# A gated mix of attention and a GeGLU layer: the softmax shift as a bias column, the branch turned round, and the first Q loads on another queue

## The chip, the core and the metric

The kernel runs on one core of a Trainium2 chip. The metric is the device time of one execution in microseconds, the median of three runs. A profile of one execution comes beside it, with a start and a duration for each instruction.

## What is computed

```python
x = A_x                                     # 2048 tokens x 512
# A: 32 heads of 16, one key and value head that all share
q = (x @ wq).reshape(1, 2048, 32, 16).transpose(0, 2, 1, 3)
k, v = x @ wk, x @ wv                       # 2048 x 16 each
p = softmax(einsum("bhqd,bkd->bhqk", q, k) * 16 ** -0.5)
a = einsum("bhqk,bkd->bhqd", p, v).transpose(0, 2, 1, 3).reshape(1, 2048, 512) @ wo
# B: 512 -> 1376 -> 512
b = (gelu(x @ w_gate) * (x @ w_up)) @ w_down
g = sigmoid((x * gate_w).sum(-1, keepdims=True))
out = g * a + (1 - g) * b
```

All of it is float32. `wq` and `wk` are drawn eight times larger than the other weights.

## The kernel before

Every float32 operand of the projections is split into a high and a low part of a 32-bit matmul type, and each product is made of three passes (high by high, low by high, high by low).

**Start.** For each of four groups of 512 tokens, TensorE makes the keys, values and the gate's dot product in one pass (`pk`) and the queries in four blocks of 128 rows (`pq`). `post_k` writes the keys into `kp`, `post_v` the values into `v1` and `v2`, and `post_q` writes each block of queries, high and low, to a scratch tensor `scr` in memory (L213, on SyncE's queue). VectorE keeps the largest absolute value of queries (`qmx`) and keys (`kmx`).

**Scores.** One unit `u` covers four heads over 512 tokens. `load_q` loads the unit's queries from `scr` into a tile `Q`, in two halves of partitions, 64 apart, for two heads that run side by side: 48 rows of queries (high, low, high) against 48 rows of keys (high, high, low). Behind them stand QK - KR = 3 further rows, loaded from a second scratch tensor `shs` (L285): two for a row shift in two parts, which are zero on the usual path, and a row of ones. The rows of `kp` against them are ones, ones, and a constant row. So the score matmul contracts 51 rows, and the constant row adds one number to every score. Each of the 1024 exponentials (L579) then reads a 128x1024 tile of scores in PSUM with an immediate scale and an immediate bias of 0.0.

**The shift and the branch.** `pairmax` multiplies the two maxima to a bound on the scores (`cb`), sets `flag` where the bound is over a limit, and spreads -1.01 times the bound over a row of 2048 numbers on VectorE (L318), which two transfers on ScalarE's queue (L320) put into `kp` as the constant row. The engines load `flag` (L518) and branch on it (L519). The body, for large scores, finds each row's true maximum over all scores, and puts it into `shs`; it is not entered with these inputs. A body of some 2100 TensorE instructions in the program's order, with over 1000 of VectorE and some 200 of SyncE, stands between the comparison and the code behind the join. The block of the other path holds, on TensorE and VectorE, one wait for the engine's own work, and on SyncE eight waits for all outstanding transfers, each with an addition to the semaphore, so that both paths leave the same counts.

**Attention and the GeGLU layer.** Behind the branch, an order written out by hand (`WORDS`) mixes the two. `S` and `Z` make the scores of one exponential, `V` multiplies four 128x512 tiles of exponentials by the values (L649), `F` is one step of the layer's matmuls (L358, gate and up or down projections), `H` begins a job of them and `R` ends it. Scores go through three pairs of PSUM banks: `S` uses the first two in turn, `Z` the third, which the layer's gate product `z` also uses. Exponentials are kept in twelve tiles `p`. Weights of the layer come from memory on SyncE's queue (L227), and VectorE and GpSimd split them (L127, L128). The GELU is a chain of VectorE operations (L383, L386, L387), a tanh on ScalarE (L390), and further operations on VectorE (L393 to L400). The first chunk of the layer (`g` and `u`, L343) runs ahead of the branch, beside `pairmax`.

The first two units' queries are loaded inside the start (L307), on ScalarE's queue; all later ones on SyncE's.

Of the kernel before, what the change touches and what calls it, by code (L numbers as in the profile page):

```python
# [9 lines left out]
F32 = mybir.dt.float32  # L10
F32R = mybir.dt.float32r
BF16 = mybir.dt.bfloat16
I32 = mybir.dt.int32
AF = mybir.ActivationFunctionType
ALU = mybir.AluOpType
# [4 lines left out]
P = 128  # L20
S = 2048
D = 512
H = 32
DH = 16
F = 1376
TG = 512
NTG = S // TG
# [2 lines left out]
NF = -(-F // P)  # L30
NB = 4
KR = 48
QK = 51
SCALE = DH ** -0.5
BOUND = 120.0
GC = 0.044715
# [23 lines left out]
def mix_kernel(ctx, tc, xT, wq, wkv, wo, wf, out):  # L60
    nc = tc.nc
    cp = ctx.enter_context(tc.tile_pool(name="cp", bufs=1))
    dr = ctx.enter_context(tc.tile_pool(name="dr", bufs=1, space=DRAM))
# [6 lines left out]
    def two_banks(name, i=None):  # L70
        if i is None:
            i = turn[0]
        turn.remove(i)
        turn.append(i)
        return ps_s.tile([P, 2 * TG], F32, tag=f"s{i}", name=name)

    scr = dr.tile([NTG, NB, 32, 8, TG], F32, name="scr")
    shs = dr.tile([NTG, 3, H, TG], F32, name="shs")

    kp = cp.tile([P, S], F32R, name="kp")  # L80
    v1 = cp.tile([P, NKC, 32], F32, name="v1")
# [8 lines left out]
    mm2 = cp.tile([P, 2], F32, name="mm2")  # L90
    mm1 = cp.tile([1, 2], F32, name="mm1")
    cb = cp.tile([1, 1], F32, name="cb")
    sh = cp.tile([1, 1], F32, name="sh")
    flag = cp.tile([1, 1], I32, name="flag")
    woh = cp.tile([P, NB, D], F32R, name="woh")
# [68 lines left out]
        nc.gpsimd.memset(mkb[32 * j : 32 * j + 32], 1.0)  # L164
        nc.gpsimd.memset(mkb[32 * j : 32 * j + 16], 0.0)
    make_identity(nc, ident)
    zz = woh[0:H]
    nc.gpsimd.memset(zz.bitcast(F32), 0.0)
    nc.gpsimd.memset(zz[:, 2].bitcast(F32), 1.0)
    for g in range(NTG):  # L170
        nc.gpsimd.dma_start(shs[g].rearrange("r h q -> h r q"), zz[:, 0:3].bitcast(F32))

    def passes(ps, lh, ll, rh, rl, n, first=True, last=True):
        seq = [(i, a, b) for i in range(n) for a, b in ((lh, rh), (ll, rh), (lh, rl))]
# [93 lines left out]
    Q = {}  # L268
# [6 lines left out]
            q.dma_start(t[64 * j : 64 * j + 32].bitcast(F32), scr[g, b, 0:32, hs])  # L275
            q.dma_start(t[64 * j + 32 : 64 * j + KR].bitcast(F32), scr[g, b, 0:16, hs])

    def load_q(u, shift=True, data=True, q=nc.sync):
        g, ub = divmod(u, 8)
        if data:  # L280
            Q[u] = cp.tile([P, 2, TG], F32R, tag="Q", name=f"Q{u}", bufs=2)
            load_qk(Q[u], u, q)
        if shift:
            for j in range(2):
                q.dma_start(Q[u][64 * j + KR : 64 * j + QK].bitcast(F32), shs[g, :, 4 * ub + j : 4 * ub + 4 : 2])  # L285

    fetch_w(0)
    fetch_w(1)
    for ti, tg in enumerate(order):
        xh, xl = xs[tg]  # L290
        pk = ps_a.tile([P, TG], F32, tag="pa", name=f"pk{tg}")
        passes(pk, lambda c: wkh[:, c], lambda c: wkl[:, c], lambda c: xh[:, c], lambda c: xl[:, c], NC)
        post_k(tg, pk)
        for b in range(NB):
            pq = two_banks(f"pq{tg}_{b}")[:, 0:TG]
            bs = slice(b * P, (b + 1) * P)
            passes(pq, lambda c: wqh[:, c, bs], lambda c: wql[:, c, bs], lambda c: xh[:, c], lambda c: xl[:, c], NC)
            if ti + 1 < NTG:
                split_x(order[ti + 1], b)
            post_q(tg, b, pq, ti == NTG - 1 and b == NB - 1)  # L300
            if ti == NTG - 1 and b == 0:
                for part in split_w(0):
                    part()
            if ti == NTG - 1 and b == 1:
                post_v()
            if ti == NTG - 1 and b >= 2:
                load_q(b - 2, q=nc.scalar)  # L307

    def pairmax():
        pm = two_banks("pm")[0:1, 0 : 2 * P]  # L310
        for j in range(2):
            nc.tensor.transpose(pm[:, j * P : (j + 1) * P], mm2[:, j : j + 1], ident)
        nc.vector.tensor_reduce(mm1, pm.rearrange("o (j p) -> o j p", j=2), axis=AX, op=ALU.max)
        nc.vector.tensor_mul(cb, mm1[:, 0:1], mm1[:, 1:2])
        nc.vector.tensor_scalar(flag, cb, BOUND / DH, None, op0=ALU.is_gt)
        nc.vector.tensor_scalar(sh, cb, -1.01 * DH, None, op0=ALU.mult)
        row = zz[0:1].rearrange("p a b -> p (a b)")
        nc.vector.tensor_scalar(row, row, 0.0, sh[0:1], op0=ALU.mult, op1=ALU.add)  # L318
        for r in (QK - 1, 64 + QK - 1):
            nc.scalar.dma_start(kp[r : r + 1].bitcast(F32), row.bitcast(F32))  # L320

    acc = {}
    O = {}
# [17 lines left out]
    def chain_mm(ps, terms, first=True, last=True):  # L341
        for q, (a, b) in enumerate(terms):
            nc.tensor.matmul(ps, a, b, start=(first and q == 0), stop=(last and q == len(terms) - 1),  # L343
                             skip_group_check=True)
# [29 lines left out]
    def weights_terms(n, t):  # L374
        gh, gl = W[n][:2]
        xh, xl = xs[chunks[n][0]]
        return [(w[:, t, c], x[:, c]) for c in range(NC) for w, x in ((gh, xh), (gh, xl), (gl, xh))]
# [119 lines left out]
    def run_later():  # L497
        for s in sorted(later):
            if s <= now[0]:
                for fn in later.pop(s):  # L500
                    fn()

    ps = ps_f.tile([P, TG], F32, tag="pf", name="g0")
    terms = weights_terms(0, 0)
# [1 line left out]
    pairmax()  # L506
    chain_mm(ps, terms[9:], first=False)
    up0 = ps_a.tile([P, TG], F32, tag="pa", name="u0")
    chain_mm(up0, weights_terms(0, 1))
    gelu(0, ps, lambda: up0)  # L510
    rest = split_w(1)
    for part in rest[:2]:
# [3 lines left out]
    base = now[0] + 1  # L516

    v = nc.values_load(flag[0:1, 0:1], min_val=0, max_val=1)  # L518
    with tc.If(v > 0):  # L519
        with tc.tile_pool(name="gp", bufs=1) as gp:  # L520
            zr = gp.tile([1, S], F32, name="zr")
            nc.vector.memset(zr, 0.0)
            for r in (QK - 1, 64 + QK - 1):
                nc.sync.dma_start(kp[r : r + 1].bitcast(F32), zr)
            for g in range(NTG):
                mx = gp.tile([P, 4, H, 2], F32, tag="mx", name=f"mx{g}")
                for ub in range(8):
                    t = gp.tile([P, 2, TG], F32R, tag="gq", name=f"gq{g}_{ub}", bufs=2)
                    load_qk(t, 8 * g + ub, nc.sync)
                    for i in range(4):  # L530
                        for h in range(4):
                            rs = slice(64 * (h % 2), 64 * (h % 2) + KR)
                            for e in range(2):
                                ps = two_banks("gs")
                                for j in range(2):
                                    k0 = e * 1024 + j * 512
                                    nc.tensor.matmul(ps[:, j * 512 : (j + 1) * 512],
                                                     t[rs, h // 2, i * P : (i + 1) * P],
                                                     kp[rs, k0 : k0 + 512], start=True, stop=True)
                                nc.vector.tensor_reduce(mx[:, i, 4 * ub + h, e : e + 1], ps, axis=AX, op=ALU.max)  # L540
                m1 = gp.tile([P, 4, H], F32, tag="m1", name=f"m1{g}")
                nc.vector.tensor_reduce(m1, mx, axis=AX, op=ALU.max)
                pt = ps_f.tile([P, TG], F32, tag="pf", name=f"pt{g}")
                for i in range(4):
                    nc.tensor.transpose(pt[0:H, i * P : (i + 1) * P], m1[:, i], ident)
                nm = gp.tile([H, TG], F32, tag="nm", name=f"nm{g}")
                nb = gp.tile([H, 3, TG], F32R, tag="nb", name=f"nb{g}")
                nc.vector.tensor_scalar(nm, pt[0:H], -1.0, None, op0=ALU.mult)
                nc.vector.memset(nb[:, 2].bitcast(F32), 1.0)
                nc.vector.tensor_copy(nb[:, 0], nm)  # L550
                nc.vector.tensor_sub(nb[:, 1], nm, nb[:, 0])
                nc.sync.dma_start(shs[g].rearrange("r h q -> h r q"), nb.bitcast(F32))
            load_q(0, data=False)
            load_q(1, data=False)


# [5 lines left out]
    def scores(n, third):  # L562
        s, pr = divmod(n, 2)
        if s >= nsteps:
            now[0] += 1
            run_later()
            return
        u, kc = divmod(s, NKC)
        now[0] = base + n
        if pr == 0 and kc == 2 and u >= 1 and u + 1 < 8 * NTG:  # L570
            load_q(u + 1)
        run_later()
        ps = two_banks("s", 2 if third else next(i for i in turn if i < 2))
        for j in range(2):
            rs = slice(64 * j, 64 * j + QK)
            nc.tensor.matmul(ps[:, j * TG : (j + 1) * TG], kp[rs, kc * P : (kc + 1) * P],  # L576
                             Q[u][rs, pr], start=True, stop=True)
        p = m2.tile([P, 2 * TG], F32, tag="p", name="p", bufs=PB)
        nc.scalar.activation(p, ps, AF.Exp, bias=0.0, scale=SCALE)  # L579
        pb[s, pr] = p  # L580

    def norm(u):
# [136 lines left out]
    g = NTG - 1  # L719
# [50 lines left out]
```

## Time and profile before

| | |
|---|---|
| median of 3 runs | 1263.01 us (1261.27 to 1263.29) |
| the profiled execution: its span, the only time that its page gives | 1262.1 us |
| TensorE busy | 1248.1 us, 99% of the span, 9884 matmuls |
| ScalarE busy | 1031.1 us, 82% |
| VectorE busy | 572.8 us, 45% |
| GpSimd busy | 221.7 us, 18% |
| the 1024 exponentials (L579) | 979.8 us busy, 1025 ns each |
| mean granted TensorE clock | 0.996 |

In the lines of the profile, PE is TensorE's matmuls, PEld its weight loads, DVE VectorE, ACT ScalarE, POOL GpSimd, SP SyncE; a `q` behind the name is the engine's sequencer or its DMA queue. Groups of instructions have their line, engine, operation, tiles and shapes and count, then busy time in us and the mean of one in ns, then the idle time of the engine ahead of them and what ended it. Rows of the timeline have start and duration in us, and in brackets the idle time before. Matmuls are pipelined and their ends modelled, so a busy TensorE is not TensorE at its peak.

### The profile page before, as it was taken

How to read it: one execution, taken by the hardware profiler on the slowest of the kernel's cores; microseconds unless marked ns; L12 is line 12 of the kernel's file. 1: busy time of each engine (PE TensorE's matmuls, PEld its weight loads, DVE VectorE, ACT ScalarE, POOL GpSimd, SP SyncE). 2: the span in 40 equal slices, each digit the busy share in tenths (PEclk: the TensorE clock that was granted, in tenths of full speed). 3: DMA queues.
4: the chain of work that ended last, by engine and by line, in shares of the span. 5: the costliest groups of instructions: out<-in, count | busy, mean ns of one | idle time of the engine just before them, and what ended most of it. 6: DMA issues, size and time to landing. Idle time of an engine off the chain costs nothing.

```text
span 1262.1 us, 23901 instructions
## 1 busy us (share of the span) xinstructions
PE 1248.1 (99%) x9884; PEld 669.8 (53%) x9884; DVE 572.8 (45%) x860; ACT 1031.1 (82%) x1118; POOL 221.7 (18%) x261
## 2 busy tenths in 40 slices
PE   9989999999999999999999999999999999999998
PEld 6855555555455555545555555554544555455454
DVE  6762352635453163453546146362546324445334
ACT  5358888888898888888888888888887888888893
POOL 3132211201320020211131012120232002112100
PEclk9989999999999999999999999999999999999999
DMA  8441111111210111211030021011111013011000
GB/s 316 163 159 56 40 42 49 39 39 56 81 39 14 63 61 39 64 39 56 23 97 2 31 81 64 16 63 39 47 53 63 15 31 106 22 43 39 15 1 34
DMA packets 26371, 72.67 MB, mean 58 GB/s; under 512 B 4016, under 2 KB 4048, under 8 KB 26256
## 3 DMA queue, kind: packets, MB, share of 16 engines
q1 hardware_dynamic: 25244, 69.17, 16.5%
q8 instruction: 80, 1.31, 0.4%
q10 hardware_dynamic: 756, 1.11, 0.3%
q0 software_dynamic: 256, 0.79, 0.2%
q14 instruction: 35, 0.29, 0.1%
HBM read 57.67 MB, written 13.37 MB: 56 GB/s over the span
## 4 chain that ended last, share of the span: by engine, by line
PE 92%; ACT 1%; DVE 1%; issue 0%; POOL 0%; ACTq 0%
PE acc L649 37%; PE s L576 23%; PE z L358 18%; PE y L358 13%; ACT p L579 1%; PE wos L343 1%; DVE acc L466 0%; PE wof L343 0%; DVE sq L386 0%; POOL mark L366 0%; DVE sq L387 0%; DVE gs L394 0%; DVE n L600 0%; DVE gs L383 0%; ACT sq L390 0%
## 5 line engine op out<-in xcount | busy, mean ns | idle before, releaser
L579 ACT ACTIVATE p<-s 128x1024 f32<-128x1024 f32 x1024 | 979.8, 1025 | 176.2 <-PE s L576 169.0
L649 PE MATMUL acc<-p,v 128*32 128x512 f32 x4096 | 490.8, 598 | 0.0
L576 PE MATMUL s<-Q,kp 51*128 51x512 f32 x2048 | 392.2, 420 | 5.9 <-SPq L519 3.2
L576 PEld LDWEIGHTS s<-Q,kp 51*128 51x128 f32 x2048 | 188.1, 185 | 247.9 <-ACT p L579 167.5
L649 PEld LDWEIGHTS acc<-p,v 128*32 128x32 f32 x4096 | 107.7, 109 | 246.7 <-issue 241.1
L128 POOL TENSOR_TENSOR gl<-st,gh 128x512 fp32r<-128x512 f32 x88 | 123.9, 1429 | 400.1 <-PE s L576 177.4
L383 DVE COPY gs<-z 128x512 f32<-128x512 f32 x43 | 29.8, 692 | 247.6 <-PE z L358 124.6
L358 PE MATMUL y<-xh,gh 64*128 64x512 f32 x344 | 138.9, 404 | 1.5 <-DVE gs L394 1.5
L358 PE MATMUL z<-xh,gh 64*128 64x512 f32 x344 | 139.0, 404 | 0.7 <-POOL mark L366 0.7
L358 PE MATMUL z<-xl,gh 64*128 64x512 f32 x344 | 135.7, 394 | 0.0
L358 PE MATMUL y<-xl,gh 64*128 64x512 f32 x344 | 135.5, 394 | 0.0
L358 PE MATMUL y<-xh,gl 64*128 64x512 f32 x344 | 135.2, 393 | 0.0
L358 PE MATMUL z<-xh,gl 64*128 64x512 f32 x344 | 135.1, 393 | 0.0
L366 POOL MEMSET mark<- 1x1 f32 x81 | 8.5, 104 | 585.6 <-PE y L358 583.6
L456 DVE SCALAR_TENSOR_TENSOR acc<-z,gc,acc 128x512 f32<-128x512 f32 x24 | 18.0, 751 | 146.5 <-PE z L358 106.0
L358 PEld LDWEIGHTS z<-xh,gh 64*128 64x128 f32 x344 | 64.6, 188 | 16.0 <-POOL mark L366 8.8
L358 PEld LDWEIGHTS z<-xh,gl 64*128 64x128 f32 x344 | 64.3, 187 | 8.9
L358 PE MATMUL z<-dh,hh 64*128 64x512 f32 x176 | 69.0, 392 | 0.0
L358 PE MATMUL z<-dh,hl 64*128 64x512 f32 x176 | 68.9, 392 | 0.0
L358 PE MATMUL y<-dh,hh 64*128 64x512 f32 x176 | 68.9, 391 | 0.0
L358 PE MATMUL y<-dh,hl 64*128 64x512 f32 x176 | 68.8, 391 | 0.0
L358 PEld LDWEIGHTS z<-xl,gh 64*128 64x128 f32 x344 | 64.8, 188 | 7.6
(147 smaller groups left out, 1583.4 us busy)
## 6 DMA issues: line engine op xcount, KB each, us to landing
st<-wf SPq DMA_DIRECT2D x44, 768.0 KB
scr<-q SPq DMA_DIRECT2D x16, 512.0 KB
Q<-scr SPq DMA_DIRECT2D x60, 128.0 KB
out<-acc SPq DMA_DIRECT2D x16, 256.0 KB
Q<-scr SPq DMA_DIRECT2D x60, 64.0 KB
xr<-xT SPq DMA_DIRECT2D x6, 512.0 KB
xst<-xT SPq DMA_DIRECT2D x12, 256.0 KB
xr<-xT SPq DMA_DIRECT2D x4, 256.0 KB
```

What stands on the lines that cost most here:

```text
L128: eng_l.tensor_sub(lo, src, hi)
L343: nc.tensor.matmul(ps, a, b, start=(first and q == 0), stop=(last and q == len(terms) - 1), skip_group_check=True)
L358: mm = nc.tensor.matmul(ps, a[rs], b[rs], start=(half == 0 and q == 0), stop=(half == 1 and q == len(X) - 1), skip_group_check=True)
L366: relay = nc.gpsimd.memset(mark, 0.0).ins
L383: nc.vector.tensor_copy(gs, g)
L456: nc.vector.scalar_tensor_tensor(o, ps, w, o, op0=ALU.mult, op1=ALU.add)
L576: nc.tensor.matmul(ps[:, j * TG : (j + 1) * TG], kp[rs, kc * P : (kc + 1) * P], Q[u][rs, pr], start=True, stop=True)
L579: nc.scalar.activation(p, ps, AF.Exp, bias=0.0, scale=SCALE)
L649: nc.tensor.matmul(accp[u][32 * j : 32 * j + 32], vt[:, kc], pb[s, j // 2][:, (j % 2) * TG : (j % 2 + 1) * TG], start=(kc == 0), stop=(kc ...
```

## The change

It has three parts.

1. The shift leaves the keys. QK goes from 51 to 50, `shs` and the loads from it have two rows instead of three, and the row operation L318 and the two transfers L320 are gone. `pairmax` computes one number `sh`, already scaled; a new function `spread` multiplies a row of 128 ones by it on TensorE, which puts it on all partitions of a PSUM tile, and VectorE copies it to a 128x1 tile `bias`. `spread` stands behind nine of the twelve matmuls of `u0`. The exponentials read `bias` instead of the immediate 0.0. In the body the rows of zeros are replaced by clearing `bias`.
2. The branch is asked to fall through to the block of the false case. In the program's order this block now stands directly behind the comparison, and the body behind it.
3. The first two units' Q loads are issued on SyncE's queue, as the later ones are.

```diff
-QK = 51
+QK = 50
...
-    shs = dr.tile([NTG, 3, H, TG], F32, name="shs")
+    shs = dr.tile([NTG, 2, H, TG], F32, name="shs")
...
+    ones = cp.tile([1, P], F32, name="ones")
+    bias = cp.tile([P, 1], F32, name="bias")
...
-    zz = woh[0:H]
+    nc.gpsimd.memset(ones, 1.0)
+    zz = woh[0:H, 0:2]
     nc.gpsimd.memset(zz.bitcast(F32), 0.0)
-    nc.gpsimd.memset(zz[:, 2].bitcast(F32), 1.0)
     for g in range(NTG):
-        nc.gpsimd.dma_start(shs[g].rearrange("r h q -> h r q"), zz[:, 0:3].bitcast(F32))
+        nc.gpsimd.dma_start(shs[g].rearrange("r h q -> h r q"), zz.bitcast(F32))
...
             if ti == NTG - 1 and b >= 2:
-                load_q(b - 2, q=nc.scalar)
+                load_q(b - 2)
...
-        nc.vector.tensor_scalar(sh, cb, -1.01 * DH, None, op0=ALU.mult)
-        row = zz[0:1].rearrange("p a b -> p (a b)")
-        nc.vector.tensor_scalar(row, row, 0.0, sh[0:1], op0=ALU.mult, op1=ALU.add)
-        for r in (QK - 1, 64 + QK - 1):
-            nc.scalar.dma_start(kp[r : r + 1].bitcast(F32), row.bitcast(F32))
+        nc.vector.tensor_scalar(sh, cb, -1.01 * DH * SCALE, None, op0=ALU.mult)
+
+    def spread():
+        pm = two_banks("ps")[:, 0:1]
+        nc.tensor.matmul(pm, ones, sh, start=True, stop=True)
+        nc.vector.tensor_copy(bias, pm)
...
-    chain_mm(up0, weights_terms(0, 1))
+    terms = weights_terms(0, 1)
+    chain_mm(up0, terms[:9], last=False)
+    spread()
+    chain_mm(up0, terms[9:], first=False)
     gelu(0, ps, lambda: up0)
...
-    with tc.If(v > 0):
+    with tc.If(v > 0, preferred_fallthrough_block=False):
         with tc.tile_pool(name="gp", bufs=1) as gp:
-            zr = gp.tile([1, S], F32, name="zr")
-            nc.vector.memset(zr, 0.0)
-            for r in (QK - 1, 64 + QK - 1):
-                nc.sync.dma_start(kp[r : r + 1].bitcast(F32), zr)
+            nc.vector.memset(bias, 0.0)
...
-        nc.scalar.activation(p, ps, AF.Exp, bias=0.0, scale=SCALE)
+        nc.scalar.activation(p, ps, AF.Exp, bias=bias, scale=SCALE)
```

The lines left out make the tiles of the body two rows instead of three, and drop two arguments of `load_q` that are no longer used.

More of the change, by code (lines that the diff above doesn't have):

```diff
@@ L276, in load_qk, with load_q @@
             q.dma_start(t[64 * j + 32 : 64 * j + KR].bitcast(F32), scr[g, b, 0:16, hs])
-    def load_q(u, shift=True, data=True, q=nc.sync):
+    def load_q(u, data=True):
         g, ub = divmod(u, 8)
+        q = nc.sync
         if data:
@@ L282, in load_q @@
             load_qk(Q[u], u, q)
-        if shift:
-            for j in range(2):
-                q.dma_start(Q[u][64 * j + KR : 64 * j + QK].bitcast(F32), shs[g, :, 4 * ub + j : 4 * ub + 4 : 2])
+        for j in range(2):
+            q.dma_start(Q[u][64 * j + KR : 64 * j + QK].bitcast(F32), shs[g, :, 4 * ub + j : 4 * ub + 4 : 2])
     fetch_w(0)
```

3 lines of the change are left out of this document (1 added, 2 removed).

## The prediction

> **What bounds the kernel now.** I read the page first, then the list of waits, then busy time by stage, then the timeline.
>
> ```profile
> PE 1248.1 (99%) x9884; PEld 669.8 (53%) x9884; DVE 572.8 (45%) x860; ACT 1031.1 (82%) x1118; POOL 221.7 (18%) x261
> PE 92%; ACT 1%; DVE 1%; issue 0%; POOL 0%; ACTq 0%
> L579 ACT ACTIVATE p<-s 128x1024 f32<-128x1024 f32 x1024 | 979.8, 1025 | 176.2 <-PE s L576 169.0
> L576 PEld LDWEIGHTS s<-Q,kp 51*128 51x128 f32 x2048 | 188.1, 185 | 247.9 <-ACT p L579 167.5
> ```
>
> TensorE is busy nearly all the time and carries 92% of the chain that ended last (second line), with ScalarE at 1%. That looks like a kernel in which ScalarE, at 82%, has room. The list of waits says how thin the room is:
>
> ```profile
> ACT p L579 <- PE s L576: 169.0, 240, 8.2
> PEld s L576 <- ACT p L579: 167.5, 215, 1.2
> ```
>
> ScalarE waits for scores 240 times in 1024 exponentials, and the weight loads of the scores wait for an exponential 215 times, since a score bank is free again only once its exponential has read it. So the lead passes back and forth: 1024 / 240 = 4.27 exponentials make one streak without a wait for scores, and 215 waits against 240 streaks is about one wait of TensorE in each. By stage (us, then busy time of PE, PEld, DVE, ACT, POOL with counts, granted clock, DMA):
>
> ```profile
> 69.50:82.00 12.50, 7.96 (x42) 7.00 (x44) 6.26 (x12) 5.54 (x7) 4.19 (x4) 0.73 0.45 137
> 82.00:1262.00 1180.00, 1172.56 (x9562) 611.10 (x9558) 517.13 (x767) 996.80 (x1063) 201.54 (x222) 1.00 0.14 46
> ```
>
> The first row is the stage around the branch, the second the attention. The change touches the first by its branch, and the second by one operand of each exponential. What a streak looks like:
>
> ```profile
> 88.05 5.58 ACT L579 ACTIVATE p<-s 128x1024 f32<-128x1024 f32 x6
> 93.82 2.90 ACT L579 ACTIVATE p<-s 128x1024 f32<-128x1024 f32 x3 [0.19 <-PE s L576]
> 97.30 2.96 ACT L579 ACTIVATE p<-s 128x1024 f32<-128x1024 f32 x3 [0.59 <-PE s L576]
> ...
> 90.02 0.30 PEld L576 LDWEIGHTS s<-Q,kp 51*128 51x128 f32 x4 [1.18 <-ACT p L579]
> 93.22 0.19 PEld L576 LDWEIGHTS s<-Q,kp 51*128 51x128 f32 x2 [0.84 <-ACT p L579]
> ```
>
> In the streak of six TensorE waits for ScalarE, the last time at 93.22, behind the fifth exponential; in the two streaks of three it does not. Longer exponentials would there pass on the addition of 5 in 12.
>
> **Part 1: the bias becomes an operand in memory.** In the program of before, each exponential carries its bias as an immediate 0.0; in the changed one it reads `bias`, a 128x1 tile in SBUF. The removed key row saves nothing: a score matmul streams the same 512 columns with 50 rows as with 51. No activation of before reads such an operand, so its price is bounded by neighbours:
>
> ```profile
> L383 DVE COPY gs<-z 128x512 f32<-128x512 f32 x43 | 29.8, 692 | 247.6 <-PE z L358 124.6 <-PE y L358 123.0
> L454 DVE TENSOR_SCALAR acc<-z,gc 128x512 f32<-128x512 f32 x8 | 6.0, 751 | 51.8 <-PE z L358 51.8
> L394 DVE SCALAR_TENSOR_TENSOR gs<-y,sq 128x512 f32<-128x512 f32 x43 | 29.8, 692 | 4.0
> L456 DVE SCALAR_TENSOR_TENSOR acc<-y,gc,acc 128x512 f32<-128x512 f32 x24 | 17.8, 743 | 0.0
> L194 DVE COPY v<-pv 128x256 f32<-128x256 f32 x1 | 0.4, 408 | 0.0
> L702 DVE TENSOR_SCALAR gt<-gt 128x16 f32<-128x16 f32 x1 | 0.2, 176 | 0.0
> L700 ACT ACTIVATE gt<-zt 128x16 f32<-128x16 f32 x1 | 0.2, 207 | 0.0
> L390 ACT ACTIVATE sq<-sq 128x512 f32<-128x512 f32 x44 | 27.7, 629 | 1.2 <-DVE sq L387 1.1
> ```
>
> On VectorE the same size costs 692 ns with immediates (L383, L394) and 751 or 743 ns where a column of scalars is read (L454, L456): 55 ns more. To carry that over I scale by the fixed cost of an instruction. By the 16-element rows that is 207 ns on ScalarE against 176: 55 x 207 / 176 = 65 ns. By the slope between two sizes it is 629 - 512 x (1025 - 629) / 512 = 233 ns on ScalarE against 408 - 256 x (692 - 408) / 256 = 124 on VectorE: 55 x 233 / 124 = 103 ns. I take the middle, 84 ns. The outer ends are 0 (fetched under the instruction before) and 207 ns (a whole fixed cost again); a gain is excluded, since an operand is added. *The Trainium skill, page "ScalarE: Activation LUTs", section "What ACT_TABLE_LOAD costs", prices an ACTIVATE with immediates at 186 ns + 0.833 ns an element and adds about 93 ns for each [128,1] pointer operand. For 1024 elements the first figure gives 1039 ns, the trace has 1025; no run here shows the second. By 93 ns the sum below would be 1307.0.*
>
> All of it does not reach the end. 1024 x 0.084 = 86 us is less than the 1180.00 - 996.80 = 183 us in which ScalarE is idle in the attention stage, so ScalarE does not become the bound everywhere. An addition passes on only as far as the last place in a streak at which TensorE waits; behind it ScalarE's own wait absorbs it. The 215 waits say one such place in each streak but not where; I take the middle: 215 x 4.27 / 2 = 459 exponentials, 45% (the window above has 42%). **459 x 0.084 = 38.6 us.** A place a third into the streak gives 306 exponentials, two thirds gives 612. An addition of 4.27 x 0.084 = 0.36 us for each streak against a mean idle of 169.0 / 240 = 0.70 us joins some streaks, which speaks for the upper half.
>
> **Part 2: the branch.** The rows of the branch's line, engine by engine (count, ns, start):
>
> ```profile
> L519 DVEq COMPARE_BRANCH  x1: 72/72/72, 68.1 to 68.1; - x1
> L519 PEldq COMPARE_BRANCH  x1: 3892/3892/3892, 68.1 to 68.1; - x1
> L519 SPq COMPARE_BRANCH  x1: 45/45/45, 68.4 to 68.4; - x1
> ...
> L519 SPq EVENT_SEMAPHORE  x8: 17/17/17, 71.7 to 72.5; - x8
> L519 DVEq EVENT_SEMAPHORE  x1: 21/21/21, 71.3 to 71.3; - x1
> L519 PEldq EVENT_SEMAPHORE  x1: 51/51/51, 72.1 to 72.1; - x1
> ```
>
> On engines with a long body the jump takes 3.9 us (TensorE), 71.3 - 68.1 = 3.2 us (VectorE) and 71.7 - 68.4 = 3.3 us (SyncE). In the program's order the jump over the body stays: before, the comparison jumps to the other block, which stands behind the body; after, it falls into that block, but the block ends in an unconditional branch, and the body still lies between it and the code that follows. What moves is the wait. That block holds, on TensorE and VectorE, a wait for the engine's own work: now done after the jump, then ahead of it.
>
> ```profile
> L312 PE MATMUL pm<-ident,mm 128*1 128x128 f32 x2 | 0.4, 272 | 0.0
> ...
> 69.11 0.39 PE L343 MATMUL u<-xh,gl 128*128 128x512 f32 x1
> 72.65 0.70 PE L576 MATMUL s<-Q,kp 51*128 51x512 f32 x2 [3.15 <-SPq L519]
> ...
> 73.67 0.43 PE L358 MATMUL y<-xh,gl 64*128 64x512 f32 x1
> 75.49 0.80 PE L576 MATMUL s<-Q,kp 51*128 51x512 f32 x2 [1.39 <-issue]
> ```
>
> Before, TensorE's jump began at 68.1, under queued matmuls that ran to 69.50. After, it begins at 69.50 plus some 0.2 for the new matmul of `spread` (an estimate from the two small ones on L312, 0.4 us together) and ends at 69.7 + 3.9 = 73.6; with 0.4 us of waits behind it, taken from 72.1 to the matmul at 72.65 without the wait for SyncE, the first scores come at 74.0: **+1.3 us**. Ends: 0 (if part of the 3.9 us was itself a wait for the queue to drain) and 1.7. The stall of 1.39 us at 75.49 and the half clock after it move along at no change.
>
> ```profile
> L318 DVE TENSOR_SCALAR woh<-woh,sh 1x2048 fp32r<-1x2048 f32 x1 | 1.3, 1274 | 0.1
> ...
> 68.85 0.74 DVE L127 CAST gh<-st 128x512 fp32r<-128x512 f32 x2
> 71.45 0.76 DVE L127 CAST dh<-st 128x512 fp32r<-128x512 f32 x1 [1.87 <-DVEq L519]
> 72.85 1.67 DVE L387 SCALAR_TENSOR_TENSOR sq<-sq,gs 128x512 f32<-128x512 f32 x1
> ...
> 76.32 1.03 ACT L579 ACTIVATE p<-s 128x1024 f32<-128x1024 f32 x1 [1.15 <-PE s L576]
> 81.62 0.76 DVE L127 CAST gh<-st 128x512 fp32r<-128x512 f32 x2
> ```
>
> VectorE loses the 1.27 us row operation (L318), but its copy to `bias` waits for `spread`, which stands behind nine of the twelve u matmuls; queued behind it are the copy of g, the splits of `gh` on which GpSimd waits, and the jump. With `spread` three matmuls of 0.23 us ahead of the end of u, so near 68.8, the copy of `bias` at about 69.1, then 0.69 and 0.74 us, they end near 70.5 instead of 68.85 + 0.74 = 69.59, and VectorE resumes at 70.5 + 3.2 = 73.7 instead of 71.45.
>
> `sq` then ends at 74.52 + 2.3 = 76.8 and the tanh at 77.4; the second exponential waits for its scores until 76.3 + 1.3 = 77.6 anyway. Without that cover of 0.2 us the rest would be added. The Q loads, twelve transfers, leave ScalarE's queue, where nothing computes then, and stand on SyncE's behind and ahead of the last `scr` write; SyncE takes them, then the flag, then waits until all have landed, before 73.6 by the old chain, which ended before 72.65 with two key-row transfers more. SyncE then jumps, so the next weight loads start some 3 us later than before; they are first read at 81.62, eight microseconds behind the join: nothing.
>
> **Sum.** The profiled span is 1262.1, the median 1263.01 of runs from 1261.27 to 1263.29; 0.9 lies around the span, and I add to the median: 1263.0 + 38.6 + 1.3 = **1302.9**.
>
> **Rivals.** *The idle absorbs it*: the operand is fetched under the instruction before, or the 86 us fit into ScalarE's 183 us. For: the chain's 1%. Against: the 215 waits of TensorE on ScalarE. Then 1263.0 + 1.3 = 1264.3.
>
> *ScalarE paces everything*: all streaks join and every exponential counts: 1263.0 + 86 + 1.3 = 1350. For it the idle would have to lie where no lead can be kept; against it stand the streaks of three above, with idle time between them.
>
> ```profile
> 75.50:78.00 2.50, 2.50 (x12) 2.50 (x13) 2.21 (x4) 1.03 (x1) 0.00 (x0) 0.50 0.92 263
> 78.00:80.50 2.50, 2.50 (x14) 2.50 (x13) 0.00 (x0) 1.36 (x2) 0.00 (x0) 0.50 0.39 159
> ```
>
> *Faster, the jump goes*: if the fall-through spares the long jump, TensorE waits only for the Q loads: until about 71.5, an estimate from SyncE's first semaphore of the join at 71.7, 1.15 us sooner; the 1.39 us stall goes, and the half clock, 5.0 us of work at a granted clock of 0.50, gives back 2.5 us. That is 1263.0 - 5.0 = 1258, and it decides only if the operand costs under 5.0 / 459 = 11 ns. Against it: the body still has to be jumped. *The Trainium skill, page "Runtime: NRT & Kernel Launch", section "Instruction fetch mechanics", says that a taken branch out of the two pages held forces a fetch by DMA before execution goes on; the 3.9 us above agree, and by that rule an unconditional jump over the same body pays again.*
>
> **Chances.** Forecast 0.84, absorbed 0.08, all on ScalarE 0.06, faster 0.02. The forecast's range: 65 ns on 306 exponentials, 19.9 us, gives 1283; 103 ns on 612, 63.0, with 1.7 at the branch gives 1328. I leave out the rivals and a little of the forecast, about 0.2. A measurement of this kernel tells 0.2%, 2.5 us, from no change. Faster 0.02; same 0.07, the absorbed case nearly whole; slower 0.91.
>
> **What would show it.** Right: L579's mean at about 1109 ns instead of 1025, ScalarE's busy time up by some 86 us, its idle before L579 well under 176.2, more waits of the score loads for ScalarE, and the first scores near 74.0. Wrong: a mean still at 1025 (part 1 falls); a mean up but the span not (the absorption is complete); or no compare-and-jump gap near 70 to 73 us (part 2 falls).

## The result, and the profile after

The changed kernel takes 1284.42 us, median of 5 runs (1283.90 to 1286.47), against 1263.01 for the kernel before (5 runs, 1260.49 to 1263.29): 21.4 us slower. The ratio, taken over all runs, is 1.018 (95% interval 1.0167 to 1.0192); that of the two medians is 1.017. The forecast was 1302.9 us, in a range from 1283 to 1328. The direction and the two places were as forecast; the larger term came out at a little over half its size.

The page of the changed kernel: busy time and share of the engines, the chain that ended last, and the exponential's group with the idle time of ScalarE ahead of it; below them, from the list of waits, the two waits between TensorE and ScalarE (us, times, longest).

```profile
PE 1268.3 (99%) x9886; PEld 660.6 (52%) x9886; DVE 571.0 (45%) x860; ACT 1110.9 (87%) x1118; POOL 221.0 (17%) x261
PE 91%; ACT 1%; DVE 1%; issue 0%; POOL 0%; DMA 0%; ACTq 0%; POOLq 0%
L581 ACT ACTIVATE p<-s,bias 128x1024 f32<-128x1024 f32 x1024 | 1063.3, 1118 | 117.5 <-PE s L578 114.5
```

```profile
PEld s L578 <- ACT p L581: 233.4, 457, 1.4
ACT p L581 <- PE s L578: 114.5, 194, 9.6
```

Each exponential takes 1118 ns instead of 1025. ScalarE's busy time rose by 1110.9 - 1031.1 = 79.8 us, its idle time before the exponential fell from 176.2 to 117.5 us, and by the list of waits the weight loads of the scores wait for it 457 times, where it had 215. The chain still gives ScalarE 1%, though ScalarE's instruction is what grew. By stage (length, then busy time of PE, PEld, DVE, ACT and POOL with counts, granted clock, DMA share, GB/s):

```profile
69.50:82.00 12.50, 8.63 (x42) 6.35 (x44) 5.68 (x10) 5.76 (x7) 4.05 (x4) 0.59 0.37 134
82.00:1282.70 1200.70, 1192.08 (x9562) 602.29 (x9558) 517.23 (x767) 1076.48 (x1063) 202.19 (x222) 1.00 0.13 45
```

The attention stage grew from 1180.00 to 1200.70 us with the same 1063 instructions on ScalarE: nearly all of the loss. ScalarE's idle time in it was 1180.00 - 996.80 = 183.2 us and is now 1200.70 - 1076.48 = 124.2 us. So of 79.7 us of added work 59 went into idle time, and 20.7 came out as time. The traced execution of the kernel before has a stretch at half clock in this stage (the row below, with a granted clock of 0.50) that the changed kernel's and most others here don't have:

```profile
957.95:961.36 3.41, 3.41 (x20) 2.66 (x18) 3.41 (x4) 1.77 (x3) 3.03 (x2) 0.50 0.00 0
```

The exponentials of the traces without it gain about 1.55 us on those of before at that place, so that the stage of before is longer by this much than theirs would be, and the growth without it is 22.3 us. What the prediction showed as three streaks reads now:

```profile
88.19 9.18 ACT L581 ACTIVATE p<-s,bias 128x1024 f32<-128x1024 f32 x9
97.74 3.13 ACT L581 ACTIVATE p<-s,bias 128x1024 f32<-128x1024 f32 x3 [0.37 <-PE s L578]
101.30 2.12 ACT L581 ACTIVATE p<-s,bias 128x1024 f32<-128x1024 f32 x2 [0.44 <-PE s L578]
```

The streak of six and the next one of three have joined to nine. From its start to that of the streak behind it are 9.55 us, where it was 97.30 - 88.05 = 9.25: nine exponentials with 0.093 us each more, 0.84 us, moved the next streak by 0.30. The idle of 0.19 us between the two streaks is gone, and 0.22 of the 0.59 us before the third. Where the time stands on TensorE, by the score matmuls' group (busy, mean | idle), before and after:

```profile
L576 PE MATMUL s<-Q,kp 51*128 51x512 f32 x2048 | 392.2, 420 | 5.9 <-SPq L519 3.2 <-issue 1.4 <-ACT p L579 1.3
```

```profile
L578 PE MATMUL s<-Q,kp 50*128 50x512 f32 x2048 | 410.3, 437 | 7.0 <-SPq L525 3.8 <-ACT p L581 2.5 <-issue 0.6
```

18.1 us more busy and 1.1 us more idle, together 19.2. So the loss stands in hardly any idle column, and the page shows TensorE at 99% in both kernels. Score matmuls come in two lengths: nearly all those of over 0.45 us (0.49 us on average) start together with a weight load of the scores, which had not been done ahead, and the others take 0.39 us. Counted in the traces from 82 us on, 512 of some 2036 are long in the kernel before, 926 in the changed one. They run in pairs, so that 207 more pairs at 0.1 us each are about 20.7 us (an estimate, since the ends of matmuls are modelled).

Around the branch: the rows of its line by engine (count, shortest, median and longest ns, first and last start), then TensorE's, VectorE's and ScalarE's timeline (start, duration, in brackets the idle time before).

```profile
L525 SPq EVENT_SEMAPHORE  x8: 17/17/17, 71.6 to 72.1; - x8
L525 PEldq COMPARE_BRANCH  x2: 95/1730/3364, 66.5 to 69.1; - x2
L525 DVEq COMPARE_BRANCH  x2: 51/53/55, 68.7 to 69.6; - x2
L525 PEldq EVENT_SEMAPHORE  x1: 51/51/51, 68.9 to 68.9; - x1
```

```profile
68.51 0.40 PE L346 MATMUL u<-xh,gl 128*128 128x512 f32 x1
72.73 0.89 PE L578 MATMUL s<-Q,kp 50*128 50x512 f32 x2 [3.83 <-SPq L525]
73.42 0.62 PE L361 MATMUL y<-xh,gh 64*128 64x512 f32 x1
75.54 0.80 PE L578 MATMUL s<-Q,kp 50*128 50x512 f32 x2 [0.64 <-issue]
```

```profile
68.04 0.16 DVE L323 COPY bias<-ps 128x1 f32<-128x1 f32 x1 [2.21 <-PE ps L322]
72.44 0.43 DVE L129 CAST dh<-st 128x512 fp32r<-128x512 f32 x1 [2.98 <-issue]
```

```profile
75.19 0.63 ACT L393 ACTIVATE sq<-sq 128x512 f32<-128x512 f32 x1 [0.36 <-DVE sq L390]
76.38 1.11 ACT L581 ACTIVATE p<-s,bias 128x1024 f32<-128x1024 f32 x1 [0.56 <-PE s L578]
```

On TensorE the comparison now takes 95 ns, the wait for its own work ends at 68.9, at the end of u, and only then an unconditional branch (the longer of the two COMPARE_BRANCH rows) begins at 69.1 and takes 3364 ns. VectorE, too, compares and jumps. TensorE's gap is 3.83 us instead of 3.15. The clock: 0.59 over these 12.5 us is 2 x 0.41 x 12.5 = 10.3 us at half, where before 0.73 was 6.8 us.

### The profile page after: what moved, and what is told of

It reads as the page before. It is cut to its first block, busy times and chain, and to the rows that moved or that the text cites. A ratio compares the mean times of both kernels' runs of the same rounds, so it can differ in the third digit from the quotient of the medians.

```text
span 1282.7 us, 23905 instructions
## 1 busy us (share of the span) xinstructions
PE 1268.3 (99%) x9886; PEld 660.6 (52%) x9886; DVE 571.0 (45%) x860; ACT 1110.9 (87%) x1118; POOL 221.0 (17%) x261
## 4 chain that ended last, share of the span: by engine, by line
PE 91%; ACT 1%; DVE 1%; issue 0%; POOL 0%; DMA 0%; ACTq 0%; POOLq 0%
PE acc L651 36%; PE s L578 24%; PE z L361 17%; PE y L361 13%; ACT p L581 1%; PE wos L346 1%; DMA xst<-xT 0%; DVE acc L469 0%; POOL gl L130 0%; PE wof L346 0%; DVE ol L627 0%; DVE xh L129 0%; POOL xl L130 0%; DVE sq L389 0%; DVE sq L390 0%
## 5 line engine op out<-in xcount | busy, mean ns | idle before, releaser
L581 ACT ACTIVATE p<-s,bias 128x1024 f32<-128x1024 f32 x1024 | 1063.3, 1118 | 117.5 <-PE s L578 114.5
L578 PE MATMUL s<-Q,kp 50*128 50x512 f32 x2048 | 410.3, 437 | 7.0 <-SPq L525 3.8
L578 PEld LDWEIGHTS s<-Q,kp 50*128 50x128 f32 x2048 | 186.0, 184 | 300.6 <-ACT p L581 233.4
L361 PE MATMUL z<-dh,hl 64*128 64x512 f32 x176 | 68.9, 392 | 0.0
L361 PE MATMUL y<-dh,hl 64*128 64x512 f32 x176 | 68.9, 392 | 0.0
L361 PE MATMUL z<-dh,hh 64*128 64x512 f32 x176 | 68.8, 391 | 0.0
```

Source lines behind the costliest of these rows:

```text
L361: mm = nc.tensor.matmul(ps, a[rs], b[rs], start=(half == 0 and q == 0), stop=(half == 1 and q == len(X) - 1), skip_group_check=True)
L581: nc.scalar.activation(p, ps, AF.Exp, bias=bias, scale=SCALE)
```

## The experiments

All times are medians; each set shares its runs of the kernel before. "Ratio" is against that kernel over all runs, so that it can differ a little from that of the two medians.

| kernel | what it is | us | before | ratio, 95% interval |
|---|---|---|---|---|
| ptr_only | before, a zero tile as bias | 1283.31 | 1261.88 | 1.0167, 1.0153 to 1.0181 |
| after_imm | after, immediate 0.0 as bias | 1265.19 | 1261.88 | 1.0023, 1.0013 to 1.0033 |
| ptr_half | zero tile in every second exponential | 1266.14 | 1261.88 | 1.0035, 1.0023 to 1.0048 |
| ptr_double | tiles for bias and scale | 1332.61 | 1261.88 | 1.0558, 1.0544 to 1.0572 |
| ptr_ffn | zero tile where the layer's work follows | 1270.33 | 1261.43 | 1.0074, 1.0060 to 1.0088 |
| ptr_attn | zero tile in the others | 1269.55 | 1261.43 | 1.0066, 1.0052 to 1.0080 |
| branch_only | before, fall-through turned round | 1263.30 | 1261.43 | 1.0015, 1.0006 to 1.0024 |
| q_only | before, first Q loads on SyncE | 1265.93 | 1261.43 | 1.0038, 1.0024 to 1.0051 |
| no_shift | before without any shift | 1264.36 | 1261.66 | 1.0018, 1.0009 to 1.0027 |
| no_shift_q | no_shift, first Q loads on SyncE | 1263.35 | 1261.66 | 1.0007, 0.9998 to 1.0016 |
| fill_only | before, 12 matmuls ahead of the jump | 1263.03 | 1261.66 | 1.0013, 1.0004 to 1.0022 |
| no_shift_fill | no_shift with the 12 matmuls | 1265.16 | 1261.66 | 1.0031, 1.0021 to 1.0042 |

**The operand alone, and all but the operand.**

```diff
# ptr_only, against before
+    zb = cp.tile([P, 1], F32, name="zb")
+    nc.gpsimd.memset(zb, 0.0)
-        nc.scalar.activation(p, ps, AF.Exp, bias=0.0, scale=SCALE)
+        nc.scalar.activation(p, ps, AF.Exp, bias=zb, scale=SCALE)
# after_imm, against after
-        nc.scalar.activation(p, ps, AF.Exp, bias=bias, scale=SCALE)
+        nc.scalar.activation(p, ps, AF.Exp, bias=0.0, scale=SCALE)
```

> The kernel before, with one edit: the exponentials read a 128x1 tile of zeros as bias instead of the immediate 0.0; the key row, the branch and the Q loads stay as before. Theory A, the operand carries the whole change: L579-type exponentials at 1118 ns as in the changed kernel, time 1263 + 20 to 22 us. Rival B, branch and Q loads carry a part: under 1263 + 17 us.

> The changed kernel with the immediate 0.0 back as bias of the exponentials; bias is still computed and not read, so no shift is applied on the usual path (exp of unshifted scores). Theory A: exponentials at 1025 ns and a time within 1.5 us of 1263, since the branch, by the two traces, moves nothing by 82 us. Rival B: 1266 or more, the part that branch and Q loads cost. Prediction's part 2 by itself: 1264.3.

The exponential's group in ptr_only, then in after_imm, and after_imm's TensorE around the branch:

```profile
L581 ACT ACTIVATE p<-s,zb 128x1024 f32<-128x1024 f32 x1024 | 1063.3, 1119 | 117.1 <-PE s L578 113.6 <-ACT p L581 0.5 <-PE y L360 0.5
```

```profile
L581 ACT ACTIVATE p<-s 128x1024 f32<-128x1024 f32 x1024 | 980.6, 1025 | 176.3 <-PE s L578 159.7 <-DVE sq L389 9.6 <-ACT p L581 0.8
```

```profile
69.35 0.40 PE L346 MATMUL u<-xh,gl 128*128 128x512 f32 x1
73.53 0.89 PE L578 MATMUL s<-Q,kp 50*128 50x512 f32 x2 [3.79 <-issue]
```

The operand alone makes 1.67 of the 1.8%, with the group's mean within one nanosecond of the changed kernel's; whose tile it is doesn't matter. Theory A holds there. Without the operand the rest of the change costs 0.23%, 2.9 us, which is between what the two theories had (up to 1264.5, from 1266), and TensorE's gap of 3.79 us at the branch is there as in the changed kernel. (0.0167 and 0.0023 add up to 0.019; the changed kernel has 0.018, within the intervals.)

**The dose.** ptr_half gives the tile to every second exponential; ptr_double gives a second tile, for the scale, to all.

```diff
# ptr_half
+        nc.scalar.activation(p, ps, AF.Exp, bias=zb if n % 2 else 0.0, scale=SCALE)
# ptr_double
+    nc.gpsimd.memset(sc, SCALE)
+        nc.scalar.activation(p, ps, AF.Exp, bias=zb, scale=sc)
```

> The kernel before; every second exponential reads the tile of zeros as bias, the others the immediate. Theory linear (a fixed share of 22% of each addition passes on): + 10 us. Theory convex (the idle behind each streak takes a small addition first): + 4 to 7 us. The prediction's share of 45% would give + 21 us.

> The kernel before; all exponentials read both the bias (zeros) and the scale from 128x1 tiles. If a second operand costs as much as the first, 1211 ns each. Theory linear: + 41 us. Theory convex: the first 93 ns ate 59 us of ScalarE's 183 us of idle, the second finds less to eat, + 55 to 75 us. If the second operand is read beside the first at no cost, 1118 ns and + 21 us.

Groups by form, the attention stage and the weight loads' wait of ptr_half; the exponential's and the score matmuls' group and the stage of ptr_double:

```profile
L581 ACT ACTIVATE p<-s,zb 128x1024 f32<-128x1024 f32 x512 | 572.6, 1118 | 48.9 <-PE s L578 45.8 <-ACT p L581 0.4
L581 ACT ACTIVATE p<-s 128x1024 f32<-128x1024 f32 x512 | 525.7, 1027 | 93.0 <-PE s L578 91.6 <-PE y L360 0.6 <-ACT p L581 0.2
```

```profile
82.00:1264.30 1182.30, 1173.81 (x9548) 606.34 (x9544) 515.98 (x765) 1032.37 (x1062) 201.23 (x222) 1.00 0.14 46
```

```profile
PEld s L578 <- ACT p L581: 160.3, 279, 1.6
```

```profile
L583 ACT ACTIVATE p<-s,zb,sc 128x1024 f32<-128x1024 f32 x1024 | 1147.7, 1209 | 80.9 <-PE s L580 75.3 <-PE y L362 0.5 <-ACT p L583 0.2
L580 PE MATMUL s<-Q,kp 51*128 51x512 f32 x2048 | 430.4, 449 | 21.0 <-ACT p L583 8.4 <-SPq L523 3.1 <-issue 0.4
```

```profile
82.00:1330.80 1248.80, 1225.90 (x9550) 595.89 (x9547) 516.02 (x765) 1160.23 (x1062) 200.22 (x222) 1.00 0.14 43
```

The price is a property of the single instruction: 1118 and 1027 ns side by side, and the second tile adds another 1209 - 1119 = 90 ns. The time isn't proportional to it. ScalarE's added work in the stage is 35.6, 79.7 and 163.4 us (half, changed kernel, double), and ScalarE's idle time falls from 183.2 to 149.9, 124.2 and 88.6. The time of the stage rises by 2.3, 20.7 and 68.8; with the 1.55 us at half clock that only the trace of before has, by some 3.9, 22.3 and 70.4. The share that comes out as time is then 11% of the first 36 us, 42% of the next 44 and 57% of the next 84.

**Where an exponential stands.** ptr_ffn gives the tile to the 543 exponentials behind which a layer's step (`F`, `H` or `R`) comes, ptr_attn to the other 481.

```diff
# ptr_ffn (ptr_attn: not in)
+            ctx[0] = (toks[at + 1 : at + 2] or ["V"])[0][0]
+        nc.scalar.activation(p, ps, AF.Exp, bias=zb if ctx[0] in "FHR" else 0.0, scale=SCALE)
```

> The kernel before; the tile of zeros is read as bias by the 543 exponentials whose word is followed by a step of the layer's matmuls (F, H or R), the other 481 keep the immediate. Theory V (ScalarE paces where values and scores stand close together): + 0 to 4 us, less than half of the 21.4. Rival F (S F3 costs TensorE 0.99 us per exponential against 0.92 on ScalarE, so there the room is smallest): + 10 us or more.

> The counterpart: the 481 exponentials followed by V, S or Z read the tile of zeros, the 543 others the immediate. Theory V: + 8 to 16 us, most of the 21.4. Rival F: + 0 to 4 us. If neither place matters and only the load does (theory convex alone): both about + 4 to 5 us, as for every second exponential.

The stage and the weight loads' wait in ptr_ffn, then in ptr_attn:

```profile
82.00:1267.30 1185.30, 1177.28 (x9540) 602.99 (x9536) 515.29 (x764) 1034.86 (x1061) 200.39 (x221) 1.00 0.14 45
```

```profile
PEld s L579 <- ACT p L582: 208.0, 382, 1.4
```

```profile
82.00:1267.80 1185.80, 1177.33 (x9540) 606.32 (x9537) 515.32 (x764) 1030.56 (x1060) 200.30 (x221) 1.00 0.14 45
```

```profile
PEld s L579 <- ACT p L582: 186.2, 290, 1.7
```

Both theories fall: the two sets cost the same, 0.74% and 0.66%. But each costs about twice what ptr_half does (0.35%, intervals apart), with about as many slow exponentials, so that the third guess, that only their number counts, falls too. What differs is that here the slow ones are neighbours: in ptr_half each stands alone, in ptr_ffn all but 7 and in ptr_attn all but 64 have a slow one beside them. That additions pass on where they pile up within a few exponentials, because the three pairs of score banks give a lead of two or three, fits this and the convex dose; it is argued from these times, and no run varied the number of banks.

**The branch, and the queue.**

```diff
# branch_only, against before
-    with tc.If(v > 0):
+    with tc.If(v > 0, preferred_fallthrough_block=False):
# q_only, against before
-                load_q(b - 2, q=nc.scalar)
+                load_q(b - 2)
```

> The kernel before with the fall-through of the branch alone turned. Prediction's part 2: the wait for the engine's own work stands ahead of the jump, first scores 1 to 1.4 us after TensorE's gap would have ended, time + 1 to 3 us. Rival, the jump goes: - 3 to - 5 us and no gap of 3 us.

> The kernel before with the first two units' Q loads on SyncE's queue alone; branch, key row and immediate as before. Theory: 0 within 1 us, since the transfers land before the jump is over either way; ScalarE's two key-row transfers then start right behind pairmax instead of behind the Q loads. Rival: the loads land later and the first scores with them, + 1 to 2 us.

branch_only: TensorE's branch rows and its timeline. q_only: SyncE's queue (the transfers' issues), what its wait ended on, and TensorE's first scores.

```profile
L519 PEldq COMPARE_BRANCH  x2: 95/1780/3464, 67.4 to 68.9; - x2
```

```profile
68.35 0.39 PE L343 MATMUL u<-xh,gl 128*128 128x512 f32 x1
72.77 0.74 PE L576 MATMUL s<-Q,kp 51*128 51x512 f32 x2 [4.03 <-DVE dh L127]
```

```profile
67.25 0.77 SPq L276 DMA_DIRECT2D Q<-scr  x1
71.91 0.30 SPq L275 DMA_DIRECT2D Q<-scr  x1
```

```profile
SPq L275 <- DMA kp<-woh: 3.9, 1, 3.9
```

```profile
77.58 1.06 PE L576 MATMUL s<-Q,kp 51*128 51x512 f32 x2 [8.78 <-SPq L519]
```

Turned round alone, the branch costs 0.15%, 1.9 us, and TensorE's gap is 4.03 us instead of 3.15. In the two traced executions, which have the same stretches at half clock up to there, the last exponentials start only 0.3 us apart, so the traces show less of a loss than the medians do. The Q loads alone cost 0.38%, 4.8 us, which none of the theories had: SyncE issues nothing from 68.0 to 71.9, while its load waits 3.9 us for a key-row transfer of ScalarE's queue (`kp<-woh`), and the first scores come at 77.58.

**Without the shift.** no_shift removes the row, its transfers and its VectorE operations and adds nothing: 50 rows, immediate 0.0. It leaves out the common shift, which cancels in the softmax. no_shift_q moves the Q loads in it.

```diff
# no_shift, against before (no_shift_q: also load_q(b - 2))
-QK = 51
+QK = 50
-        nc.vector.tensor_scalar(row, row, 0.0, sh[0:1], op0=ALU.mult, op1=ALU.add)
-        for r in (QK - 1, 64 + QK - 1):
-            nc.scalar.dma_start(kp[r : r + 1].bitcast(F32), row.bitcast(F32))
```

> The kernel before without any shift: the immediate 0.0 as bias, no constant row in keys and queries (50 rows instead of 51), no transfer of the key rows from ScalarE's queue and no matrix product that spreads the shift; the branch and ScalarE's queue for the first Q loads are as before. It leaves out the common shift (which cancels in the softmax).
> Theory P (the operand alone costs the 21 us; what the row of the keys did before was worth little): 1262 (1259.5 to 1263.5), no more than the few tenths that the two key-row transfers and their three small VectorE operations take before the first scores, and the exponential stays at 1025 ns.
> Theory K (the key row itself costs time, by its 51st row in 900 score matmuls or by its transfers ahead of the first scores, so that moving the shift brings something that the operand's price hides): under 1259, with a score matmul mean well under 420 ns or first scores over 1 us earlier than 72.65.

> no_shift with the first Q loads on SyncE's queue, as in the changed kernel. With the key-row transfers still there, the same move alone took +4.5 us: SyncE's queue stood from 68.0 to 71.9 ahead of the third load of Q1, and the first scores came at 77.6.
> Theory L (that load waits for the semaphore that the first key-row transfer from ScalarE, issued at 67.65, is counted on; without the transfers there is nothing to wait for): within 1 us of no_shift; SyncE's Q loads are issued without a gap over 1 us until about 68.7, and the first scores come within 1 us of those of no_shift.
> Theory W (SyncE's queue itself is late: the stores of q and the Q loads on one queue): +3.5 to +5 us against no_shift, the gap before the third load is there again, first scores near 77.

no_shift's score matmuls; then SyncE's queue in no_shift_q and its and TensorE's branch rows:

```profile
L563 PE MATMUL s<-Q,kp 50*128 50x512 f32 x2048 | 392.1, 420 | 6.1 <-SPq L511 3.4 <-issue 1.6 <-ACT p L566 1.1
```

```profile
67.59 0.82 SPq L274 DMA_DIRECT2D Q<-scr  x1
68.45 0.45 SPq L273 DMA_DIRECT2D Q<-scr  x1
```

```profile
L511 PEldq COMPARE_BRANCH  x1: 4692/4692/4692, 67.7 to 67.7; - x1
L511 SPq COMPARE_BRANCH  x1: 45/45/45, 71.0 to 71.0; - x1
```

```profile
74.48 0.94 PE L563 MATMUL s<-Q,kp 50*128 50x512 f32 x2 [4.84 <-SPq L511]
```

The row brings nothing when it goes: a score matmul has 420 ns with 50 rows as with 51. Theory K falls. Theory P is right on the exponential, but no_shift is 0.18% slower than before, 0.9 us above the forecast range. Set side by side, in two traces that both have the half-clock stretch near 958 us, the exponentials of no_shift start level with those of before until the 88th (0.05 us apart) and fall behind by 1.6 us over the rest: 0.3 us at the 500th, 0.8 at the 700th. With that stretch allowed for, the other kernels with 50 rows and the immediate drift by 1.1 to 1.5 us from the 88th to the last, and those with 51 (branch_only, q_only, fill_only) by 0.4 to 0.5, so that part of the drift belongs to this execution of before. The rest is open.

In no_shift_q SyncE's loads are issued without the gap, so theory L is right on its cause: the load waited for the key-row transfer, as q_only's list of waits says too. The first scores still come at 74.48, 1.8 us behind no_shift's 72.67, because SyncE reaches its own jump only at 71.0, after the loads and the flag; the median is 1.0 us below no_shift's.

**The clock behind the jump.**

```diff
# fill_only, against before; no_shift_fill has the same
+    fill = two_banks("wz", 2)[:, 0:TG]
+    for _ in range(12):
+        nc.tensor.matmul(fill, warm[:, 0:P], warm, start=True, stop=True)
```

> The kernel before with 12 more 128x512 bf16 matmuls on a warm-up tile into a bank that is free, between the last projection matmul and the jump: TensorE's clock record has no gap of over 3 us before the first scores. It adds work whose result is not read.
> Theory H (the 6.8 us at half clock after the jump come from the 3.15 us in which TensorE has no matmul, and cost about 2.5 us net of the matmuls put in): 1260.5 (1259 to 1262), with the half clock after the jump gone or one window of 3.4 us shorter.
> Theory J (the gap is the instruction fetch of the jump itself, and comes after the fill as it came before): 1263 to 1266, the same gap of 3 us and the same half clock, shifted by the fill's length of up to 3 us.

> no_shift and fill together. Theory H with P: 1259.5 (1258 to 1262), the first scores at about the time of no_shift, and no or less half clock after them. Theory J: no_shift's time plus 0 to 3 us, half clock as before.

fill_only: TensorE's jump and the wait behind it, its timeline and the stage around the branch.

```profile
L522 PEldq COMPARE_BRANCH  x1: 3812/3812/3812, 67.8 to 67.8; - x1
L522 PEldq EVENT_SEMAPHORE  x1: 51/51/51, 71.7 to 71.7; - x1
```

```profile
68.59 2.76 PE L512 MATMUL wz<-warm 128*128 128x512 bf16 x12
75.22 0.70 PE L579 MATMUL s<-Q,kp 51*128 51x512 f32 x2 [3.86 <-issue]
```

```profile
69.50:82.00 12.50, 8.64 (x51) 6.81 (x51) 5.65 (x9) 4.93 (x7) 3.43 (x4) 0.86 0.36 131
```

Both theories are half right. The times lie where J has them, but not for J's reason: the jump begins at 67.8 us, under the fill, and is over at 71.6, so that the fill covers it, as H wants. The gap of 3.86 us comes behind it. TensorE's sequencer passes a wait at 71.87, and its next instruction stands at 75.0; in no_shift_fill it stops in the same way from 72.03 to 74.96. The kernel before has such a stop further on, the stall ahead of the second scores, which ends at 75.49. In both it ends some 3.4 us behind the end of the jump (75.0 - 71.66 and 75.49 - 72.01), but it comes behind the second instruction that the trace records after the jump instead of behind the 25th. The fill puts 24 instructions, 12 matmuls and 12 weight loads, ahead of the jump. A stop at a fixed place of the program would come earlier by about that number, and this fits; no run moved the place alone. The half clock shrinks, as H says, from 6.8 to 2 x 0.14 x 12.5 = 3.5 us; ptr_ffn, without a fill, also has 0.86 there in its traced execution, so that the traces alone don't tie this to the fill. The first exponential starts 2.6 us later than before, the seventh 0.1 us later: the two cancel, and the times are 0.13% and 0.31% above before. No version here beats the kernel before by its median.

## Why the prediction was right, and where it was off

- **The operand's price, 84 ns (65 to 103):** measured 93, by the group's means of 1025 and 1118 ns. Right; VectorE's ratio carried over low by 9 ns. *The Trainium skill, page "ScalarE: Activation LUTs", section "What ACT_TABLE_LOAD costs", has about 93 ns for each such operand: agreed to here, with 93 for the first and 90 for the second.*
- **How much passes on, 459 exponentials (306 to 612):** this is the step that failed, though the total lay in the range. 21.4 us, what ptr_only adds to its median, over 0.093 are 230 exponentials, 22%, below its lower end. That the total stayed in the range is luck: the dearer operand made up part of the lower count, since 306 x 0.065 was the low end of 19.9, and 230 x 0.093 is 21.4. The rule was that an addition passes on up to the last place in a streak at which a weight load waits for ScalarE, 215 waits being one in each streak. But most of those waits were not ended by ScalarE. The list names the releaser that came last, even where it had long been done. The window of the prediction has such a case: the fifth exponential of the streak ends at 91.66 + 1.05 = 92.71, and the weight load that is said to wait for it starts 0.5 us later, at 93.22, under the last of the value matmuls.

```profile
91.66 1.05 ACT L579 ACTIVATE p<-s 128x1024 f32<-128x1024 f32 x1
```

  The last load there that ScalarE did hold up is the one at 90.93, behind the third exponential (it ends at 90.88). Three in 12 are 25%, near the 22% measured, where the prediction read 5 in 12. Over the whole trace, of the 215 loads with such a wait only 29 start within 0.1 us of the end of the exponential, and their waits are 11.6 of the 167.5 us. In ptr_half these are 133 of 279 (37.9 us), in the changed kernel 315 of 457 (114.3 us), in ptr_double 404 of 530 (169.1 us). So the rule had TensorE held up by ScalarE about once in each streak from the start, and the runs show that this is rare at first and grows with the dose. The dose shows the same: if a fixed 45% passed on, half the operands would have cost 512 x 0.45 x 0.093 = 21 us; they cost 4.3.
- **The idle absorbs it** (rival, 1264.3): wrong as a whole, but near at half the dose, which costs 4.3 us. **ScalarE paces everything** (1350): not reached even at twice the dose, where 57% of the last addition passes on.
- **The branch, +1.3 us (0 to 1.7):** right in mechanism, and the size is not settled. The jump stays, with an unconditional branch of 3364 ns; the wait stands ahead of it. From the start of the last u matmul to the first scores there are 72.73 - 68.51 = 4.22 us instead of 72.65 - 69.11 = 3.54. The other traces agree: 3.34 to 3.75 us in the seven kernels with the branch of before and its Q loads and no fill, 4.18 to 4.42 in the three with the branch turned, some 0.7 us more. branch_only costs 1.9 us (0.8 to 3.0 by its interval), of which its trace shows 0.3 at the end. The first scores come at 72.73 instead of 74.0, though: 0.6 us because the last u matmul started that much earlier in this execution (68.51 against 69.11), and most of the other 0.7 because the unconditional branch took 3.36 us where 3.9 were carried over, so that part of the 3.9 belonged to something else, as the lower end allowed.
- **"The stall and the half clock move along at no change":** wrong in detail, without effect on the sum. The half clock lasts 10.3 us instead of 6.8 and covers the first layer matmuls too (0.62 us at 73.42, where the one at 73.67 took 0.43), but the stall of 1.39 us has shrunk to 0.64, so that the second scores come at 75.54, where they were at 75.49.
- **VectorE's late join:** as forecast in kind; `bias` is copied at 68.04 behind a wait of 2.21 us, and VectorE resumes 72.44 - 71.45 = 1.0 us later, not 2.25. Nothing waits for it: the tanh on L393 starts at 75.19 and ends before 76.38, when the second exponential has its scores.
- **The Q loads, nothing:** holds in the changed kernel, whose SyncE is at its eight semaphores by 71.6. It holds only because the key-row transfers go in the same change; q_only paid 4.8 us. The prediction had counted queues, but not that a load can wait for a transfer of another queue.
- **Faster, the jump goes:** excluded by the row of 3364 ns. *The rule of the Trainium skill, page "Runtime: NRT & Kernel Launch", section "Instruction fetch mechanics", that a taken branch out of the pages held is fetched first, agrees.*

## What to carry to other kernels

An operand in memory instead of an immediate costs each activation some time (93 ns here, at the one size that was measured); multiply it by the count, then ask how much the engine's idle time can take before calling the rest a loss. When two engines hand a lead back and forth, don't count waits by the engine that a list names: ask for each whether that engine had only just finished when the wait ended. And expect the share that passes on to rise with the dose: half of an edit may be nearly free where the whole is not. A change in three parts should be priced together as well as apart: moving the loads was free only because the transfers that they would have waited for had gone.

## What the runs showed of the hardware

- Turning a branch so that the usual path falls through doesn't save the long jump here, where the block of the other path still lies between: 95 ns for the comparison, and then 3.36 us (changed kernel) and 3.46 us (branch_only) on TensorE for the unconditional branch.
- Behind the jump TensorE's sequencer stops a second time. The stop ends at 75.49 us in the kernel before, 75.54 in the changed kernel and 75.0 in fill_only, 3.1 to 3.5 us behind the end of the jump. Covering the jump with matmuls did not cover this one.
- The half clock behind the branch comes in steps: about 3.5, 6.8 and 10.3 us, worked out from granted clocks of 0.86, 0.73 and 0.59 over 12.5 us. *The Trainium skill, page "TensorE: Matmul & The Clock Gate", section "Part 1: The HAM clock gate (the "warmup" mystery)", has a free-running window of 3413 ns; one, two and three of them are 3.4, 6.8 and 10.2 us, so the traces agree.* A gap of 3.8 us brought one window in fill_only and three in the changed kernel, and behind the same branch the kernel before had two (0.73) and ptr_ffn one (0.86): where the gap falls in the grid seems to count as much as its length.
- no_shift, with one row less in its score matmuls and otherwise the same order, drifted 1.6 us behind the kernel before over some 1070 us, about 1.0 us of it beyond what the kernels with 51 rows do. No run explains it.
